# A recurrent-memory transformer block on one core: streamed weights copied into contiguous pieces, small transfers on ACT's queue, whole-bank evictions

## The chip, the cores and the metric

One core of one Trainium2 chip. The metric is device time in microseconds (us), median of several executions. A ratio is the mean time of one kernel's runs over that of the other's runs of the same rounds, so it is not quite the ratio of the medians that are quoted.

Engines: PE does matmuls, PEld its weight loads, ACT (ScalarE), DVE (VectorE) and POOL (GpSimd) the rest; SP issues transfers. "ACTq" and "SPq" are the issuing sequencers of ACT and SP. The profile counts 16 DMA engines. A bank is here a tile of 512 columns in PSUM, into which PE's matmuls add up; to evict it is to copy it out, so that the next instructions can read it.

## The reference

```python
def reference(A_x, A_mem0, A_Wq, A_Wk, A_Wv, A_Wo, A_seg_len, B_x, B_w1, B_b1, B_w2, B_b2):
    # x: 2048 x 1024, 32 heads of 128, 8 memory rows, segments of 32 rows -> 64 segments
    def _A_ref(x, mem0, Wq, Wk, Wv, Wo, seg_len):
        mem = mem0
        for s in range(n_seg):
            h = jnp.concatenate([mem, xs], axis=1)       # 8 + 32 rows
            q, k, v = h @ Wq, h @ Wk, h @ Wv             # each weight 1024 x 4096, 8 MB
            p = _softmax(masked(q @ k.T * scale))
            o = (p @ v) @ Wo                             # 4096 x 1024, 8 MB
            mem = o[:, :M, :].copy()                     # the next segment needs it
            outs.append(o[:, M:, :])
        ...
    def _B_ref(x, w1, b1, w2, b2):
        return gelu(x @ w1 + b1) @ w2 + b2               # 1024 -> 3584 -> 1024
    xn = _layernorm(A_x)
    return A_x + _A_ref(xn, ...) + _B_ref(xn, ...)
```
(Shortened; everything is bf16.) The four weights of A have 32 MB together, more than fits on chip with the rest. The kernel keeps 43 of 64 units of 512 KB resident and reads the other 21 again in each of the 64 segments.

## The kernel before

First the feed-forward block B for all 2048 rows in four token groups, with the layer norm; it leaves x + B in DRAM (`R_d`, and `RL_d` for the last 8 rows of each segment). Then the loop over segments. In it a segment is computed for 24 of its rows and the 8 memory rows; the leftover 8 rows of four segments are collected, so in each group of four the first segment also has their K and V, the fourth their O and the next group's Q. The 16 extra stores of their output go out during the next group's first segment. (The prediction and some expectations, which counted from the stores, call this one the "fourth" kind; the tables here call it the first.)

```python
        def unit_tile(unit):
            if IS_STREAMED[unit]:
                t = stp.tile([P, 2048], BF16, name="st")[:, :]      # 4 buffers
                fetch(t, unit)                   # SP; from the weight itself
                state["n"] += 1
                if state["n"] == STREAM_BUFS:
                    for fn in later:             # small loads and stores, SP too
                        fn()
                    later.clear()
                return t
            # [... resident units ...]

        def load_h(s):
            hT = sp.tile([P, KT, SEG], BF16, name="hT", bufs=2)
            nc.sync.dma_start(out=hT[:, :, :], in_=xT_d[:, s, :].rearrange("p (k t) -> p k t", k=KT))
            return hT
        # [... load_hL, load_res, load_resL alike ...]

        def copy2(dst, src):
            nc.scalar.copy(out=dst[0], in_=src[0])
            nc.vector.tensor_copy(out=dst[1], in_=src[1])
        # [...]
            for w in ("K", "Q"):
                left = left_kv if w == "K" else left_q
                for u in range(2):               # a half pass: 8 units into one PSUM bank
                    ps, psL = half_pass(w, u, left, {3: todo})
                    nat = evict(ps, [sp.tile([P, 256], BF16, name=nm) for nm in NAT[u]])  # copy2 of two halves
                    todo = [turner(nat, "kT" if w == "K" else "qT", u)]    # PE transposes, next half pass
        # [... scores, softmax, V, O; then, of a segment's output ot: ...]
            def store(s=s, ot=ot):
                for jq in range(4):
                    nc.sync.dma_start(
                        out=out_flat[s * SEG:s * SEG + NX, 256 * jq:256 * jq + 256], in_=ot[32 * jq:32 * jq + NX, :]
                    )
            later.append(store)                  # every fourth segment 16 more, store_left
```

The streamed unit of K, Q or V is 128 rows of 4 KB at a pitch of 8 KB; a unit of O is two blocks of 128 rows of 2 KB.

The softmax here doesn't subtract the row's maximum and nothing guards it: scores larger than these inputs give would overflow.

## Time and profile before

| | before |
|---|---|
| time, median | 3075.97 us (3052.85 to 3080.03) |
| span of the profiled run | 3067.4 us |
| block B, handover, loop | 454, 28, 2585 us |
| loop: DMA share, GB/s, mean clock | 0.83, 280, 0.87 |
| segment, by place in its group of four | 44.0, 37.9, 37.3, 41.9 us |
| DMA idle in it | 11.6, 4.4, 4.4, 6.8 us |

A page line of 40 digits cuts the span into equal slices, each digit the busy share in tenths. In the views of waits a row is engine, line, what it waited for, us in total, times, longest. The view of one engine in order of time has start, us, engine, line, operation and number. Segment figures are averages over the stretches between two additions of a segment's output (`ot`), so they start in the O pass of one segment and end in that of the next. The packets' durations come from the trace's own records of DMA packets. The prediction shows the lines of before and reads them.

### The profile page before, as it was taken

To read this page: it belongs to the slowest core of one execution; us is meant where nothing else is said; L and a number is where in the kernel's file an instruction comes from. 1 tells how busy PE (TensorE), PEld (TensorE's weight loads), DVE (VectorE), ACT (ScalarE), POOL (GpSimd) and SP (SyncE) were. 2 spreads that over 40 slices of the span, in tenths; PEclk is the share of its full clock that TensorE was granted. 3 is DMA by queue.
4 is the path that set the end of the run, shared out by engine and by line. 5 is a ranking of instruction groups with operands and counts; after the bars stand their busy time and mean duration, and the time that the engine had idled before them with its cause. 6 is when DMAs were issued, how large, how long until landed. Compare 5 with 4: busy or idle time off the path is not lost.

```text
span 3067.4 us, 83824 instructions
## 1 busy us (share of the span) xinstructions
PE 2197.4 (72%) x37364; PEld 1117.2 (36%) x37387; DVE 694.9 (23%) x2203; ACT 579.8 (19%) x1520; POOL 8.7 (0%) x28
## 2 busy tenths in 40 slices
PE   5899995676766676767666766767676776776775
PEld 2344442333333333433333333434333333333333
DVE  4566421111111111111111111111111111111111
ACT  2244221111111111111111111111111111111111
POOL 0000000000000000000000000000000000000000
PEclk9999997897888889888888798998888988888888
DMA  7111267878787878888787878787978887888787
GB/s 244 47 40 44 76 224 259 293 252 291 261 289 260 288 257 301 278 280 295 271 294 249 294 263 313 259 303 255 307 262 301 272 306 253 306 269 299 259 299 256
DMA packets 307206, 779.91 MB, mean 254 GB/s; under 512 B 32667, under 2 KB 78747, under 8 KB 306332
## 3 DMA queue, kind: packets, MB, share of 16 engines
q1 hardware_dynamic: 306716, 774.53, 75.0%
q8 instruction: 292, 4.78, 0.6%
q14 instruction: 70, 0.57, 0.1%
q10 hardware_dynamic: 128, 0.02, 0.0%
HBM read 759.72 MB, written 14.68 MB: 252 GB/s over the span
## 4 chain that ended last, share of the span: by engine, by line
DMA 47%; PE 39%; SPq 5%; DVE 4%; ACT 3%; issue 2%; POOL 0%; DVEq 0%; ACTq 0%; POOLq 0%
DMA st<-in_A_Wk_dram 20%; PE acc L509 17%; DMA st<-in_A_Wv_dram 17%; PE sm L681 7%; DMA st<-in_A_Wq_dram 5%; PE ps L293 5%; PE ps L339 5%; DMA st<-in_A_Wo_dram 4%; SPq L712 2%; PE tr L451 1%; PE ps L366 1%; PE acc L652 1%; ACT rc L622 1%; DVE kv L435 1%; ACT sm L619 1%
## 5 line engine op out<-in xcount | busy, mean ns | idle before, releaser
L509 PE MATMUL acc<-st,hT 128*32 128x512 bf16 x4096 | 470.4, 444 | 580.6 <-DMA st<-in_A_Wk_dram 372.0
L509 PE MATMUL acc<-W,hT 128*32 128x512 bf16 x8192 | 793.1, 436 | 0.4 <-issue 0.4
L509 PEld LDWEIGHTS <-hT 128*32 128x32 bf16 x12288 | 363.9, 103 | 1051.3 <-issue 846.6
L509 PE MATMUL acc<-W,hL 128*32 128x512 bf16 x2048 | 220.9, 413 | 0.8 <-issue 0.8
L293 PE MATMUL ps<-xnT,w 128*128 128x512 bf16 x896 | 199.5, 385 | 17.9 <-ACT g_xb L301 16.9
L435 DVE CAST natD<-acc 128x256 bf16<-128x256 f32 x192 | 80.8, 421 | 504.5 <-ACT natC L434 503.2
L434 ACT CAST natA<-acc 128x256 bf16<-128x256 f32 x192 | 71.4, 372 | 562.7 <-PE acc L509 477.1
L435 DVE CAST natB<-acc 128x256 bf16<-128x256 f32 x192 | 81.5, 424 | 399.4 <-ACT natA L434 347.5
L434 ACT CAST natC<-acc 128x256 bf16<-128x256 f32 x192 | 71.8, 374 | 493.2 <-PE acc L509 492.8
L339 PE MATMUL ps<-w,gT 128*128 128x512 bf16 x654 | 150.8, 386 | 5.5 <-ACT g_xb L301 2.5
L293 PEld LDWEIGHTS <-w 128*128 128x128 bf16 x896 | 88.7, 99 | 127.8 <-issue 25.6
L509 PEld LDWEIGHTS <-hL 128*32 128x32 bf16 x3072 | 92.8, 104 | 81.1 <-issue 25.8
L509 PE MATMUL acc<-st,hL 128*32 128x512 bf16 x1024 | 111.1, 414 | 0.5 <-issue 0.5
L435 DVE CAST kv<-acc 128x256 bf16<-128x256 f32 x128 | 53.9, 421 | 242.6 <-ACT kv L434 234.9
L435 DVE CAST o_sb<-sm 128x128 bf16<-128x128 f32 x63 | 18.4, 291 | 398.5 <-ACT o_sb L434 398.5
L652 PE MATMUL acc<-pr,kv 32*128 32x40 bf16 x2048 | 53.7, 179 | 63.4 <-DVE pr L623 42.8
L339 PEld LDWEIGHTS <-gT 128*128 128x128 bf16 x672 | 66.3, 99 | 85.9 <-issue 3.3
L681 PE MATMUL sm<-st,natA 128*32 128x256 bf16 x1024 | 71.0, 334 | 31.2 <-ACT natA L434 30.8
L681 PE MATMUL sm<-W,natB 128*32 128x256 bf16 x1536 | 91.1, 331 | 0.0
L434 ACT CAST o_sb<-sm 128x128 bf16<-128x128 f32 x63 | 16.7, 265 | 392.1 <-PE sm L681 392.1
L301 ACT ACTIVATE g_xb<-ps,b1col 128x512 bf16<-128x512 f32 x112 | 76.5, 683 | 67.7 <-PE ps L293 67.4
L434 ACT COPY kv<-tr 128x256 bf16<-128x256 bf16 x128 | 47.6, 372 | 220.1 <-PE tr L451 220.1
(118 smaller groups left out, 2420.3 us busy)
## 6 DMA issues: line engine op xcount, KB each, us to landing
st<-in_A_Wk_dram SPq DMA_DIRECT2D x384, 512.0 KB
st<-in_A_Wq_dram SPq DMA_DIRECT2D x320, 512.0 KB
st<-in_A_Wv_dram SPq DMA_DIRECT2D x320, 512.0 KB
st<-in_A_Wo_dram SPq DMA_DIRECT2D x320, 512.0 KB
w<-in_B_w_dram SPq DMA_DIRECT2D x14, 1024.0 KB
W<-in_A_Wq_dram SPq DMA_DIRECT2D x11, 512.0 KB
W<-in_A_Wv_dram SPq DMA_DIRECT2D x11, 512.0 KB
W<-in_A_Wk_dram SPq DMA_DIRECT2D x10, 512.0 KB
```

The lines of the kernel that those rows point to most:

```text
L293: nc.tensor.matmul(ps[:, :].rearrange("p (s t) -> p s t", t=SEG), lhsT=w1_sb[fb // 4][:, kt, (fb % 4) * P:(fb % 4 + 1) * P], rhs=xnT[:, :, ...
L301: nc.scalar.activation(out=xb[:, :], in_=ps[:, :], func=ACT.Identity, bias=b1col[:, fb:fb + 1], scale=1.0)
L339: nc.tensor.matmul(ps[:, :], lhsT=gts[fc // 7][:, fc % 7, t * P:(t + 1) * P], rhs=w2_sb[fc // 4][:, fc % 4, cs], start=(fc == 0), stop=(fc ...
L366: nc.tensor.matmul(pss[2 * t + nb][:, :], lhsT=gts[fc // 7][:, fc % 7, t * P:(t + 1) * P], rhs=w2_sb[fc // 4][:, fc % 4, nb * 512:nb * 512 ...
L434: nc.scalar.copy(out=dst[0], in_=src[0])
L435: nc.vector.tensor_copy(out=dst[1], in_=src[1])
L451: nc.tensor.transpose(dst[k][:, c, :], nat[k][:, c * P:(c + 1) * P], ident[:, :])
L509: nc.tensor.matmul(acc[32 * j:32 * j + 32, :], lhsT=lhs[:, i, :], rhs=t[:, 512 * j:512 * j + 512], start=(i == 0), stop=(i == KT - 1), til ...
L619: nc.scalar.activation(out=dA, in_=dA, func=ACT.Ln)
L652: nc.tensor.matmul(oV[j][:, c, :], lhsT=V[c // 2][q, (c % 2) * P:(c % 2 + 1) * P], rhs=prA[q, c, :], start=(c == 0), stop=False, skip_grou ...
L681: nc.tensor.matmul(psX[32 * jq:32 * jq + 32, o:o + 256], lhsT=lhs[:, c, :], rhs=t[:, 1024 * k + 256 * jq:1024 * k + 256 * jq + 256], start ...
L712: nc.sync.dma_start(out=rows_o[i, NX:SEG, 256 * jq:256 * jq + 256], in_=otL[32 * jq + NL * i:32 * jq + NL * i + NL, :],)
```

## The change

Its intent: read the streamed units from contiguous memory, keep SP's queue for the stream alone, evict a bank with one engine, and take work out of the first token group.

```diff
+    copies = {
+        unit: dram.tile([P, 2048], BF16, name="Wc_" + ...) for unit in ORDER if IS_STREAMED[unit]
+    }
 # [... at the end of the first token group ...]
+                if tg == 0:
+                    for unit, c in copies.items():
+                        fetch(c[:, :], unit)
 # [... the stream ...]
             if IS_STREAMED[unit]:
                 t = stp.tile([P, 2048], BF16, name="st")[:, :]
-                fetch(t, unit)
-                state["n"] += 1
-                if state["n"] == STREAM_BUFS:
-                    for fn in later: ...
+                nc.sync.dma_start(out=t, in_=copies[unit][:, :])
 # [... load_h, load_hL, load_res, load_resL, store, store_left: nc.sync -> nc.scalar ...]
-            nc.sync.dma_start(out=hT[:, :, :], in_=xT_d[:, s, :]...)
+            nc.scalar.dma_start(out=hT[:, :, :], in_=xT_d[:, s, :]...)
 # [... one engine for a bank: K, Q, second V and memory by ACT; first V and leftovers by DVE ...]
-                    nat = evict(ps, [sp.tile([P, 256], BF16, name=nm) for nm in NAT[u]])
+                    nat = sp.tile([P, 512], BF16, name=f"nat{u}")
+                    nc.scalar.copy(out=nat[:, :], in_=ps[:, :])
+                    if (w, u) == ("K", 0):
+                        for fn in later:
+                            fn()
+                        later.clear()
 # [... block B: residual stored by rows, turned later by DRAM-to-DRAM transfers ...]
         def keep_R(ttg, rsb):
-            for i in range(4): ...        # 8 small stores a tile
+            eng = nc.scalar if ttg >= NT - 4 else nc.sync
+            eng.dma_start(out=R_n[ttg * P:ttg * P + P, :], in_=rsb[:, :])
 # [... layer-norm statistics of later rows no longer loaded and computed in the first group ...]
-                if tg == 0 and fb >= 3 and fb % 2 and 4 + fb // 2 - 1 < NT:
-                    ln_stats(tt, load_x(tt, "xst", 2))
```

## The prediction

> **What bounds the kernel now.** I read the page's 40 slices first, to separate stages, then busy time by stretch, then the waits, the groups, the chain that ended last, and the queue of SP in order of time.
>
> ```profile
> PE   5899995676766676767666766767676776776775
> DMA  7111267878787878888787878787978887888787
> q1 hardware_dynamic: 306716, 774.53, 75.0%
> DMA 47%; PE 39%; SPq 5%; DVE 4%; ACT 3%; issue 2%; POOL 0%; DVEq 0%; ACTq 0%; POOLq 0%
> ```
>
> Two stages show: up to slice 6 (about 460 us) PE is at 8 or 9 tenths and DMA nearly idle, the feed-forward block and layer norm; after it DMA is at 7 or 8 tenths all the way, the recurrent loop over 64 segments, each of which reads 21 weight units of 512 KB again. By stretch (us, busy of PE, PEld, DVE, ACT, POOL, clock, DMA share, GB/s):
>
> ```profile
> 0.00:454.00 454.00, 408.13 (x1908) 187.04 (x1931) 234.39 (x581) 151.86 (x241) 8.68 (x28) 0.97 0.35 111
> 454.00:482.00 28.00, 0.53 (x2) 0.21 (x2) 3.64 (x9) 0.00 (x0) 0.00 (x0) 0.57 0.68 193
> 482.00:3067.00 2585.00, 1788.77 (x35454) 929.98 (x35454) 456.89 (x1615) 427.97 (x1279) 0.00 (x0) 0.87 0.83 280
> ```
>
> 454 us of block, 28 us of handover in which PE does nothing, 2585 us of loop. In the loop DMA is busy 83%; the waits of PE in it say whether it is the bound:
>
> ```profile
> PE acc L509 <- DMA st<-in_A_Wk_dram: 372.0, 205, 8.4
> PE acc L509 <- DMA st<-in_A_Wv_dram: 120.0, 177, 3.0
> PE acc L509 <- DMA st<-in_A_Wq_dram: 73.1, 92, 2.3
> PE acc L652 <- DVE pr L623: 42.8, 63, 0.8
> PE sm L681 <- DMA st<-in_A_Wo_dram: 41.8, 46, 2.4
> ```
>
> 607 us of waits for streamed units, and over half of that at K, the first thing of a segment. Why K: SP's queue in order of time around one segment start (start us, us, engine, line, transfer):
>
> ```profile
> 1497.49 3.97 SPq L163 DMA_DIRECT2D st<-in_A_Wk_dram  x4
> 1502.61 1.75 SPq L699 DMA_DIRECT2D out_dram<-ot  x4
> 1504.41 0.35 SPq L414 DMA_DIRECT2D hT<-xT_d  x1
> 1505.05 0.35 SPq L424 DMA_DIRECT2D res<-R_d  x1
> 1506.31 0.32 SPq L419 DMA_DIRECT2D hL<-xL_d  x1
> 1507.67 1.87 SPq L163 DMA_DIRECT2D st<-in_A_Wk_dram  x2
> ```
>
> After four stream issues SP waits for the last segment's output, issues small stores and loads, and only at 1507.67 goes on with the stream; in 1506-1509.5 the DMA share is 0.50. Every fourth segment adds 16 small stores of about 0.33 us each. I cut the loop at the output additions and averaged by position in the group of four: segments last 44.0 (K and V of leftover rows, 16 extra stores), 37.9, 37.3 and 41.9 us (leftover Q and O), at DMA shares 0.735, 0.883, 0.881, 0.837, so DMA stands idle 11.6, 4.4, 4.4 and 6.8 us of them. PE waits for DMA 9.95, 10.3, 10.1 and 8.2 us; what is left, 34.0, 27.6, 27.2 and 33.7 us, is PE's own path with its other waits.
>
> **What the Trainium skill says.** (1) "DMA: Bandwidth & Descriptors", section "Issuing engines are not separate DMA queues": transfers started by scalar or sync run on the same 16 engines, and a second issuer saves only issue time. The trace agrees on the cost: 0.28 to 0.43 us of queue time per small transfer; here that time is on the path. (2) The same page, "Latency and other measured facts", says that a large power-of-two row pitch lowers the rate; its smallest pitch is 512 KiB, the K, Q and V units have 8 KB, so it only hints. The trace decides: its packet records give the 4096-byte packets a median of 159 ns but a mean of 192 in the loop (a tail over 300 ns); the 2048-byte packets of O, contiguous in memory, a median of 84 and, where no other weight flows, a mean of 91.4. Excess over the median is 9% for O, 19% for K, Q, V (189 ns alone). (3) "PSUM — Partial Sum Buffer", section "PSUM bank collisions raise a hardware error": two engines must not touch the same bank and quadrant together, so accesses are serialised. The trace agrees: two half evictions of one bank run one after the other, ACT 1507.05 for 0.37 us, then DVE 1507.46 for 0.42, 0.83 in all. (4) "TensorE: Matmul & The Clock Gate", Part 1: idle halves the clock. The trace agrees: stretches at 0.50, loop mean 0.87.
>
> **The change, part by part.**
> *Contiguous pieces.* The 21 units are copied once to contiguous memory, 4096 bytes a row. O's packets become 4 KB as well. If the new packets have O's relative tail, one takes 159 x 91.4/84 = 173 ns. A segment has 21 x 128 = 2688; on 16 engines 2688 x 173/16 = 29.1 us. Before: 16 x 128 x 192/16 + 5 x 256 x 94.8/16 = 24.6 + 7.6 = 32.2 us. Saving 3.1 us, on the path where DMA is the bound. Small transfers stay, about 1 us: 30.1 us of DMA a segment.
> *Copying.* 11 MB DRAM to DRAM, queued behind the loads of the first token group, in a stage where the share is 0.1 to 0.2. At half the loop's 340 GB/s (an estimate) 65 us, hidden before the next token group needs anything.
> *Small transfers on ACT's queue.* SP issues nothing but the stream, so the next unit goes out when PE frees its buffer. Of the idle DMA time, I take 2.5 us in ordinary segments, and about 7 in the fourth with its 23 issues x 0.33 = 7.6 us. Cost: 6 to 22 issues on ACT, 2 to 7 us per segment, right after the first K eviction; ACT is 17% busy in the loop and has the next half pass (about 4 us) before it is needed. In the fourth segment the second K eviction may come 3 us late; four buffers of 1.4 us each cover that.
> *Evictions.* ACT or DVE alone takes a bank of 512 columns. ACT's activation of 128x512 takes 0.69 us, against 0.83 for the serial pair: 0.15 to 0.25 us sooner at K, Q, V and at the memory hand-back. Perhaps 0.5 us of PE's path a segment, mostly behind DMA.
> *The first stage.* The 12 extra loads and statistics in the first token group go. Now DVE waits 21 us for them and PE stands from 47 to 60, then runs at DVE's pace to 111; elsewhere the same 28 blocks take 48 us (158 to 205). Starting at about 21 instead of 23, the group ends at 70 instead of 111: 40 us. Statistics of later groups (4 x 1.4 us on DVE) go beside 12 us of matmuls; the later transposes cost about 1 us three times. Net 37 us.
> *The handover.* 32 small stores of the residual (0.3 us each on SP) become 4 stores now and the rest later: additions 5 us, one store's landing, a few issues, a 2 us landing, two transposes: about 14 instead of 28 us.
>
> **Sum.** Block and handover: 482 - 37 - 14 = 431 us. Ordinary segments: DMA 30.1 plus some 1.7 left idle = 31.8 us. The two with leftovers: PE's own path, 33 to 34 now, less about 1 for evictions and a higher clock, plus some remaining DMA wait: 34.5 us, DMA and PE nearly level there. Mean 33.2. First segment 38, 63 x 33.2 = 2092, tail 8: span 2569. Times ran some 9 us above the span (3075.97 against 3067.4): 2578, which I round to 2580.
>
> **The rivals.**
> *The layout brings nothing*: the tail belongs to the 16 engines, not to the 8 KB pitch. For it: some K/Q/V stretches already reach 380 to 397 GB/s, O has a tail too. Then DMA is 2688 x 189/16 + 1 = 32.8, ordinary segments 34.5, the others 36.3, mean 35.4: 139 us more, 2715.
> *PE becomes the bound everywhere*, since its queue of waits and half-clock stretches takes over: for it, 34 us of own path in two of four segments; against, 27 in the other two. With contiguous packets at the 159 ns median, DMA needs 27.7 us, and segments fall only to 29.5 and 33.5, mean 31.5: 2470.
> *ACT becomes the obstacle*: issues block its in-order queue (single issues took up to 1.8 us on SP[...]), evictions come late and PE waits 2 us a segment more: +120 us at most, about 2700.
> *The gain is hidden anyway*: against it stands that every part concerns the wait that ends last in the loop.
>
> **Range and chances.** The rate of contiguous packets moves the result by -110 to +139 us, ACT's issues by up to +120, the first stage by 20 either way. They hardly add up: 2450 to 2720. All rivals stay more than 11% under 3076, so slower or same would need a fault that nothing here shows: faster 0.97.
>
> **What will show it.** Packet records: mean of streamed 4 KB packets near 173 ns (159 to 180 right, 189 the first rival). Loop DMA share above 0.9 and over 325 GB/s. SP's queue without gaps of small issues at the segment start; PE's wait at K far under 372 us. Segment lengths near 32, 32, 34.5, 34.5. The loop starting near 431 us. Waits of PE for ACT's evictions over 2 us a segment would speak for the third rival. The prediction fails if the copies lie badly in memory (packets slower than 192 ns), or if the clock falls under 0.85.

## More of the kernel before

One more detail is needed later, two evictions of one bank of 512 columns in order of time:

```profile
1514.36 0.37 ACT L434 CAST natC<-acc 128x256 bf16<-128x256 f32 x1 [5.16 <-PE acc L509]
...
1514.77 0.43 DVE L435 CAST natD<-acc 128x256 bf16<-128x256 f32 x1 [5.24 <-ACT natC L434]
```

DVE starts when ACT has ended: 0.84 us for a bank.

## The result, and the profile after

| | before | after |
|---|---|---|
| time, median of 4 | 3078.0 us | 2896.77 us (2891.56 to 2903.1) |
| ratio | | 0.9429 (95%: 0.9374 to 0.9484) |
| span | 3067.4 us | 2889.8 us |

Faster by 5.7%, but 177 us above the top of the predicted range. (Before was run once more beside it, hence 3078.0.) The same parts of the page:

```profile
PE   7999986566776677767676777677676767677766
...
DMA  9401378869898888988887889887989787888987
...
q1 hardware_dynamic: 230124, 769.52, 75.9%
...
DMA 49%; PE 42%; ACT 3%; DVE 2%; issue 2%; ACTq 1%; SPq 0%; DVEq 0%
```

SP's queue is gone from the chain that ended last (5% to 0), and the packets of queue 1 are fewer (306716 to 230124), as O's units now have 4 KB rows and the small transfers left. The stages:

```profile
0.00:420.50 420.50, 400.77 (x1911) 185.30 (x1931) 236.29 (x586) 157.42 (x249) 10.78 (x28) 1.00 0.44 146
420.50:440.70 20.20, 0.52 (x3) 0.14 (x2) 4.09 (x8) 1.28 (x1) 0.00 (x0) 0.59 0.80 270
440.70:2889.00 2448.30, 1724.84 (x35454) 905.20 (x35454) 387.00 (x1103) 350.59 (x831) 0.00 (x0) 0.88 0.85 296
```

The block and the handover end at 441 us instead of 482, about as predicted (431). The loop is where the forecast fell: 2448 us instead of some 2138, at a DMA share of 0.85, not over 0.9. PE's waits in it:

```profile
PE tr L455 <- ACT nat L552: 157.8, 30, 13.1
PE acc L511 <- DMA st<-Wc_Q: 145.6, 123, 4.0
PE acc L511 <- DMA st<-Wc_K: 127.4, 184, 2.3
PE acc L511 <- DMA st<-Wc_V: 76.6, 119, 2.1
PE acc L649 <- DVE pr L620: 42.8, 63, 0.8
PE sm L679 <- DMA st<-Wc_O: 40.7, 59, 2.0
```

The wait at K fell from 372 to 127 us. Two others took part of its place: the wait at Q doubled (73.1 to 145.6), and a wait of the transposes for ACT's eviction of K appeared, in 30 cases up to 13 us each. ACT in order of time at the start of a group's first segment shows what it does instead:

```profile
1369.05 0.59 ACT L552 CAST nat<-acc 128x512 bf16<-128x512 f32 x1 [4.14 <-PE acc L511]
1369.12 1.58 ACTq L697 DMA_DIRECT2D out_dram<-ot  x4
1372.46 9.51 ACTq L710 DMA_DIRECT2D out_dram<-ot  x16
1382.01 0.37 ACTq L424 DMA_DIRECT2D hT<-xT_d  x1
1382.42 0.71 ACTq L434 DMA_DIRECT2D res<-R_d  x1
1383.23 0.59 ACT L552 CAST nat<-acc 128x512 bf16<-128x512 f32 x1 [13.60 <-DMA out_dram<-ot]
```

Between the evictions of K's first and second half lie 22 issues, 14 us in place of the 7.3 that 22 issues of 0.33 us would take. In 1376 to 1383 PE does nothing. SP's queue, which now has nothing but the stream, in the same stretch:

```profile
1366.19 1.61 SPq L414 DMA_DIRECT2D st<-Wc_K  x2
1368.78 11.40 SPq L414 DMA_DIRECT2D st<-Wc_Q  x5
```

Five issues of 0.3 to 0.5 us each are spread over 11.4 us. Averages by place in the group:

| segment | us before | us after | DMA idle before | after | PE waits for ACT's eviction, after |
|---|---|---|---|---|---|
| first (leftover K, V; 16 more stores) | 43.96 | 42.63 | 11.65 | 11.09 | 8.53 |
| second | 37.91 | 36.22 | 4.45 | 3.33 | 0.85 |
| third | 37.33 | 35.13 | 4.43 | 3.62 | 0.47 |
| fourth (leftover Q, O) | 41.93 | 38.49 | 6.81 | 4.98 | 0.53 |

The idle DMA time that was to go is mostly still there. PE's waits for ACT's eviction are 157.8 us over 63 segments, 2.5 us each; over 2 was what the prediction named as the sign of its third rival. And the 4096-byte packets of the stream have a mean of 184.8 ns (192.1 before), not 173; 8.9% of them last over 1.25 of the median of 159 ns (12.9% before).

Why should SP still stand still, when it issues only the stream? The instruction list of the built program names what each instruction waits for (an excerpt, with SP's and ACT's rows from different places; the traces agree with it, see below):

```
SP:  667 st_18368<-Wc_Q_5_0_104 128x2048         [waits DMAHW5_49,DMAHW0_49,PE_49]
SP:  668 st_18385<-Wc_Q_0_1_105 128x2048         [waits DMAHW6_49,DMAHW1_49,PE_49]
ACT: 589 out_0_dram<-ot_12807 24x256             [waits DMAHW3_49,DVE_49]
ACT: 590 out_0_dram<-ot_12807 24x256             [waits DMAHW5_49]
ACT: 593 hT_12854<-xT_d_57 128x256               [waits DMAHW1_49]
```

A semaphore is a counter on which one instruction can wait until another has finished. In this built program the transfers complete on eight semaphores, DMAHW0 to DMAHW7, which the transfers of both queues use in turn. A transfer on SP waits until an earlier one on the same semaphore has landed, even if that one was issued on ACT; and ACT's wait for SP's. The trace shows the same: in the loop, SP's stream and ACT's small transfers complete on the same eight semaphores (numbers 101 to 105 and 107 to 109). In the trace of the changed kernel SP's waits in the loop contain

```profile
SPq L414 <- PE acc L511: 589.4, 713, 6.3
SPq L414 <- PE sm L679: 337.2, 297, 4.2
SPq L414 <- DMA st<-Wc_K: 211.3, 159, 4.5
SPq L414 <- DMA st<-Wc_Q: 208.3, 191, 5.4
SPq L414 <- DMA out_dram<-ot: 191.3, 83, 5.9
```

191 us of SP's waits ended with the landing of a small store. By place in the group such waits for small transfers are 7.7, 2.0, 4.8 and 2.4 us per segment; before, at most 0.2.

Not all of this waiting is loss, as SP would wait for a free buffer meanwhile. So, from the trace, how long a stream issue starts after both its buffer was free (PE's last matmul on the unit four loads back) and SP's previous stream issue was over: of 1336 issues 133 start more than 0.3 us late, 281 us together. 127 of them start within 0.15 us of a landing on the very semaphore that they use. ACT is held likewise: of its 136 pauses of 0.3 to 6 us before an issue, 131, 155 us together, end within 0.15 us of such a landing, and 70 of these landings belong to SP's stream.

**Theory A**: the slow packets belong to restarts of the stream after gaps, so the layout is worth little. **Theory B**: the two queues are coupled, by the shared semaphores and by ACT's order, in which evictions stand behind issues; that is where the expected gain went. **Rivals**: (C) the loop simply runs at the stream's own rate and PE's own path; (D) ACT's order alone is the obstacle.

### The profile page after: what moved, and what is told of

It is laid out like the page before. It is cut to its first block, busy times and chain, and to the rows that moved or that the text cites. A ratio compares the mean times of both kernels' runs of the same rounds, so it can differ in the third digit from the quotient of the medians. Undisturbed runs are those within 1.5% of the kernel's fastest.

```text
span 2889.8 us, 82618 instructions
## 1 busy us (share of the span) xinstructions
PE 2126.1 (74%) x37367; PEld 1090.6 (38%) x37387; DVE 627.4 (22%) x1696; ACT 509.3 (18%) x1081; POOL 10.8 (0%) x28
## 3 DMA queue, kind: packets, MB, share of 16 engines
q1 hardware_dynamic: 230124, 769.52, 75.9%
## 4 chain that ended last, share of the span: by engine, by line
DMA 49%; PE 42%; ACT 3%; DVE 2%; issue 2%; ACTq 1%; SPq 0%; DVEq 0%
PE acc L511 15%; DMA st<-Wc_Q 15%; DMA st<-Wc_V 13%; DMA st<-Wc_K 11%; PE sm L679 9%; PE ps L306 7%; DMA out_dram<-ot 5%; PE ps L353 5%; DMA st<-Wc_O 2%; PE tr L455 2%; PE ps L382 1%; PE acc L649 1%; ACT rc L619 1%; ACT oT L663 1%; ACT sm L616 1%
## 5 line engine op out<-in xcount | busy, mean ns | idle before, releaser
L511 PE MATMUL acc<-W,hT 128*32 128x512 bf16 x8192 | 763.8, 422 | 1.2 <-issue 1.2
L511 PE MATMUL acc<-st,hT 128*32 128x512 bf16 x4096 | 452.5, 428 | 372.1 <-DMA st<-Wc_Q 145.6
L552 ACT CAST nat<-acc 128x512 bf16<-128x512 f32 x256 | 150.1, 586 | 1242.2 <-PE acc L511 835.0
L679 PEld LDWEIGHTS <-oT 128*32 128x32 bf16 x8192 | 251.2, 109 | 132.3 <-issue 70.7
L455 PE MATMUL tr<-ident,nat 128*128 128x128 bf16 x1024 | 113.6, 241 | 158.2 <-ACT nat L552 157.8
L679 PE MATMUL sm<-W,oT 128*32 128x256 bf16 x4096 | 223.4, 315 | 3.3 <-issue 3.2
L679 PE MATMUL sm<-st,oT 128*32 128x256 bf16 x2560 | 165.5, 313 | 76.0 <-DMA st<-Wc_O 40.7
L533 DVE COPY kv<-tr 128x512 bf16<-128x512 bf16 x128 | 54.3, 424 | 651.0 <-PE tr L455 651.0
L455 PEld LDWEIGHTS <-nat 128*128 128x128 bf16 x1024 | 64.6, 105 | 280.5 <-ACT nat L552 192.0
L533 DVE COPY qT<-tr 128x512 bf16<-128x512 bf16 x128 | 54.3, 425 | 432.8 <-PE tr L455 432.8
L598 ACT ACTIVATE pr<-sm 128x448 bf16<-128x448 f32 x64 | 34.8, 544 | 298.6 <-PE sm L593 298.6
```

The costliest lines, as they stand in the source:

```text
L455: nc.tensor.transpose(dst[:, c, :], nat[:, c * P:(c + 1) * P], ident[:, :])
L511: nc.tensor.matmul(acc[32 * j:32 * j + 32, :], lhsT=lhs[:, i, :], rhs=t[:, 512 * j:512 * j + 512], start=(i == 0), stop=(i == KT - 1), til ...
L533: nc.vector.tensor_copy(out=dst[:, :, 0:32], in_=by_head(tr[:, :, :]))
L552: nc.scalar.copy(out=nat[:, :], in_=ps[:, :])
L598: nc.scalar.activation(out=pr, in_=psS[:, 0:448], func=ACT.Exp, scale=INV_SQRT_DH)
L679: nc.tensor.matmul(psX[32 * jq:32 * jq + 32, o:o + 256], lhsT=lhs[:, c, :], rhs=t[:, 1024 * k + 256 * jq:1024 * k + 256 * jq + 256], start ...
```

## The experiments

Each was timed in 3 rounds beside the kernel before, in four series on four chips; the kernel before had medians of 3075 to 3078 us in all four. Differences between two changed kernels are differences of their medians; the 95% intervals of the ratios correspond to 7 to 17 us either way. Names with "pool" have the small transfers on GpSimd.

### One part undone: no copies

```diff
-                nc.sync.dma_start(out=t, in_=copies[unit][:, :])
+                fetch(t, unit)
```
(and the copying removed)

> The changed kernel with one part undone: the stream reads the 21 units from the original weights again, there are no copies. Theory A (the tail of slow packets belongs to the moments in which the stream starts again after a gap, not to the layout): the mean of the 4096-byte packets in the loop stays between 180 and 195 ns, and only O pays for its 2048-byte packets; 20 to 80 us more than the changed kernel's 2897 us. Rival, as predicted (contiguous pieces save 3.1 us a segment): about 200 us more, near 3095 us. First stage unchanged, loop start at 440 us within 5.

Measured: 3054.09 us, 157 us more than the changed kernel (ratio to before 0.9915, 0.9877 to 0.9953). Packets of 4096 bytes 194.4 ns, those of 2048 bytes 94.1. Every kind of segment is longer by 2 to 3 us. The packets alone would have fitted theory A (180 to 195 ns), but its 20 to 80 us do not: theory A falls, and the layout is worth about four fifths of what was predicted for it (3.1 us a segment, 198 us). Part of it is packet time: 16 x 128 x 194.4/16 + 5 x 256 x 94.1/16 = 32.4 us a segment against 2688 x 184.8/16 = 31.0, so some 90 of the 157 us. The rest is not explained.

### One part undone: small transfers back on SP

```diff
-            nc.scalar.dma_start(out=hT[:, :, :], in_=xT_d[:, s, :]...)
+            nc.sync.dma_start(out=hT[:, :, :], in_=xT_d[:, s, :]...)
```
(likewise all small loads and stores of the loop)

> The changed kernel with one part undone: the small loads and stores of the loop are issued on SP again, at the places in the program where the changed kernel has them. Theory B (the move gained little, because in the built program both queues share eight completion semaphores in rotation, so SP's stream waits for the small transfers that ACT issues late, and ACT's evictions wait behind its issues): within 2% of the changed kernel, 2840 to 2950 us; the waits of PE for the eviction of K's second half fall from 8.5 us to under 2 us in every fourth segment, and DMA waits come in their place. Rival, as predicted (SP free of small issues saves 2.5 us in three segments and 7 in the fourth): 230 us more, near 3130 us.

Measured: 2992.45 us, 95 us more than on ACT. That misses theory B's 2%, and is far from the predicted 230. Segments 45.8, 36.4, 36.5, 40.3 us; no waits for ACT's evictions, PE's waits for DMA 12, 10, 10 and 7 us. So ACT's queue did bring something, less than half of the forecast. By the measure from above 70 stream issues start late, by 463 us together, and 408 us of this end when DVE has added up the output that the stores on SP's queue wait for. It is no exact return to before: the small transfers now come after three stream issues of the segment, formerly after four.

### Small transfers on GpSimd

```diff
-            nc.scalar.dma_start(out=hT[:, :, :], in_=xT_d[:, s, :]...)
+            nc.gpsimd.dma_start(out=hT[:, :, :], in_=xT_d[:, s, :]...)
```
(likewise the other small loads, the stores and the last turned residuals)

> The changed kernel with the loop's small loads and stores issued on GpSimd, whose transfers have eight completion semaphores of their own in the built program, so that neither SP's stream nor ACT's evictions wait for them. Theory B: segments fall from 42.6, 36.2, 35.1, 38.5 us to about 34, 32, 32, 34; time 2600 to 2700 us; waits of PE for ACT's eviction under 1 us in every kind of segment. Rival C (the loop is at the rate of the stream itself, packets of 185 ns and PE's own path): no more than 60 us less than the changed kernel, 2840 to 2900 us.

In the built program the small transfers now wait on other semaphores, DMASW0 to DMASW7, and the stream on DMAHW alone; in the trace GpSimd's transfers complete on numbers 111 to 118, the stream on its old eight. Measured: **2688.45 us**, ratio to before 0.8750 (0.8701 to 0.8799). Segments 34.8, 34.0, 32.7 and 36.8 us; DMA idle 3.6, 1.7, 1.8 and 3.7. The loop in the view by stretch:

```profile
441.00:2680.00 2239.00, 1656.69 (x35456) 889.37 (x35456) 387.78 (x1104) 349.95 (x831) 358.05 (x699) 0.94 0.91 324
```

SP's waits in the same kernel's loop:

```profile
SPq L414 <- PE acc L511: 621.1, 886, 3.4
SPq L414 <- PE sm L679: 343.5, 296, 3.7
SPq L414 <- DMA st<-Wc_K: 231.1, 282, 5.4
SPq L414 <- DMA st<-Wc_Q: 181.3, 254, 2.7
```

No row of this view is left for a small transfer. PE's waits for ACT's evictions of K and Q are gone too. DMA is busy 91% at 324 GB/s, PE's mean clock rose to 0.94. Rival C falls: the stream can go much faster than in the changed kernel. Of 1336 stream issues 1 now starts more than 0.3 us late, by 1.3 us (133 and 281 us in the changed kernel). This is the best of the kernels here that compute the right result, and it lies inside the range that was predicted for the changed one.

### ACT's order without the coupling of semaphores, step by step

```diff
-                    nc.scalar.copy(out=nat[:, :], in_=ps[:, :])
+                    if (w, u) == ("K", 1):            # e12: in (("K", 1), ("Q", 0))
+                        nc.vector.tensor_copy(out=nat[:, :], in_=ps[:, :])
+                    else:
+                        nc.scalar.copy(out=nat[:, :], in_=ps[:, :])
```

> The changed kernel, with K's second bank evicted by DVE instead of ACT, so that the issues on ACT no longer stand before that eviction, while the shared semaphores stay. Theory B (both count): PE's wait of 8.5 us for the eviction in every fourth segment goes, but SP's stream still waits for the small transfers, so DMA waits come in its place: 20 to 80 us less than the changed kernel. Rival D (ACT's order alone is the obstacle): 15 segments x 8 us plus some tenths in the others, 120 us or more less, under 2780 us.

Measured: 2838.17 us, 59 us less than the changed kernel. In the first segments PE still waits 3.4 us for ACT, now for Q's first half. So, with both on DVE:

> The changed kernel with K's second and Q's first bank evicted by DVE, so that PE needs nothing of ACT while it issues the small transfers; they stay on ACT and in the shared rotation of semaphores. Theory B: PE's wait for ACT's evictions falls under 1 us in the fourth kind of segment (3.4 us with K's second bank alone on DVE), and what remains over the kernel on GpSimd is the rotation: segments of 37 to 39, 35.5, 35, 38 us, time 2780 to 2835 us. Rival D (ACT's order alone): within 2% of 2688 us.

Measured: 2828.86 us (2805.27 to 2836.53). PE's waits for evictions of K or Q on ACT are 0.2 us in the first segments and none in the others. Segments 38.7, 36.1, 34.9, 38.6 us against 34.8, 34.0, 32.7, 36.8 on GpSimd. SP's waits in its loop still have the row

```profile
SPq L414 <- DMA out_dram<-ot: 203.3, 89, 5.7
```

and SP waits 9.3, 2.1, 4.8 and 1.7 us per segment for small landings. Rival D falls: of the 208 us between ACT's queue and GpSimd's, 68 go when PE no longer needs ACT's evictions of K and Q; 140 us remain. The 68 are net: with ACT's order out of the way, the stream was held longer than before, 168 issues late by 343 us together.

### Only the 16 extra stores on GpSimd

```diff
-                            nc.scalar.dma_start(
+                            nc.gpsimd.dma_start(
                                 out=rows_o[i, NX:SEG, 256 * jq:256 * jq + 256],
```

> The changed kernel with only the 16 small stores of the leftover rows issued on GpSimd; the 4 stores and 2 or 3 loads of each segment stay on ACT. Theory B: the fourth kind of segment falls from 42.6 to about 36.5 us, since only 6 issues stand before the eviction and in the rotation; the other three, which keep the shared semaphores, stay at 36, 35 and 38.5 us, not at the 34, 32.7 and 36.8 of the kernel wholly on GpSimd: 16 x 6 = 96 us less, 2780 to 2820 us. Rival: the 16 stores are the whole matter: under 2720 us.

Measured: 2796.37 us. The first segment falls from 42.6 to 35.9 us; the others stay at 36.1, 35.2 and 38.4. As expected by B: 6 or 7 small transfers on ACT still cost each of the other segments some 2 us over GpSimd's queue.

### Small transfers issued earlier on ACT

```diff
             todo = []
+            for fn in later:
+                fn()
+            later.clear()
             for w in ("K", "Q"):
```
(and removed behind K's first half pass)

> The changed kernel with the small transfers placed ahead of K's first half pass instead of behind it; all stay on ACT, which issues them some 3 us earlier and is idle then. Theory B (rotation of eight shared semaphores): now the third prefetched unit of the next segment, and those behind it, wait for stores that wait for the end of this segment, so the prefetch is cut: the ordinary segments get longer by 2 us or more (36.2 and 35.1 to over 38), the time goes over 2990 us. Rival E (what is left of the loss on ACT's queue is that both issuers share the making of descriptors, or the rings, not the semaphores): earlier issue does no harm, 2800 to 2900 us.

Measured: 2888.06 us, the same as the changed kernel within 0.3%; segments 43.3, 35.7, 34.5, 39.1. My expectation of theory B was wrong (over 2990 us), and the time is the one that was written down for rival E, something else that both issuers share, such as the rings or the making of descriptors. SP's waits for small landings are 8.5, 1.7, 1.5 and 3.9 us per segment, 241 us in all against 261: the stores are issued earlier, and what that gives at one place is lost at another. So the time of this run does not tell B's semaphores from E.

The traces do tell more. If the rings or the descriptors were what two issuers share, the stream's transfers should take longer once issued. They do not: from issue to landing their mean is 5.3 us in the changed kernel and with two evictions on DVE, 5.5 on GpSimd's queue. GpSimd's own small stores even take longer than ACT's, 4.8 us against 3.7 on average, so its gain is not that they are faster. What differs is when the stream's issues may start: late by 281 us in the changed kernel, 343 with two evictions on DVE, 197 here, and 1.3 on GpSimd, nearly all ended by a landing on the semaphore to be used. So the coupling by semaphores is shown; how many of the 140 us each late issue costs stays open, as the lateness and the time do not go in step. A kernel that keeps ACT's queue but gives it its own semaphores could not be built here.

### One part alone, on the kernel before

```diff
-            nc.sync.dma_start(out=hT[:, :, :], in_=xT_d[:, s, :]...)
+            nc.gpsimd.dma_start(...)                  # e8;  e14: nc.scalar
```
(in the kernel before, all small transfers of the loop, at their old place)

> The kernel before, with the one part of moving the loop's small loads and stores off SP, but to GpSimd instead of ACT. The prediction's term for this part was 2.5 us in three segments and 7 in the fourth, 232 us: 2846 us. If SP's small issues were not what held the stream: over 3000 us.

> The kernel before, with the one part of moving the loop's small transfers to ACT's queue, at their old place in the program. Theory B: the rotation stays shared, so little of the 216 us that GpSimd's queue brought comes: 2960 to 3080 us. The prediction's step (SP issues nothing but the stream): 2846 us, as on GpSimd.

Measured: 2860.18 us on GpSimd and **3122.53 us on ACT**, before 3075.28 and 3077.30. The predicted value of freeing SP's queue was 232 us; GpSimd's queue gives 215. ACT's queue, taken alone, makes the kernel 1.4% slower (1.0144, 1.0111 to 1.0178): clear of noise, and above the 2960 to 3080 us that I expected. In its first segments PE waits 11.5 us for copies on DVE that stand behind copies on ACT, which stand behind issues:

```profile
PE tr L451 <- DVE kv L435: 171.9, 39, 11.0
```

In the kernel before, this row has 25.1 us.

### The evictions

```diff
-                    nc.scalar.copy(out=nat[:, :], in_=ps[:, :])
+                    halves(nat, ps, 256)              # ACT the first 256 columns, DVE the others
```
(likewise V, the leftovers, the memory and the copies of the transposes)

> The kernel on GpSimd's queue, with every bank of 512 columns (and the memory hand-back) evicted in two halves by ACT and DVE again, as before the change, and the transposes copied out by both. As predicted, half a us of PE's path a segment, mostly behind DMA: 10 to 35 us more than 2688. Rival: the serial pair is on the path of the segments with leftovers, which are PE's: 60 us or more.

Measured: 2704.06 us, 16 us more than with whole banks, as predicted for this part. But it is within the noise of two kernels in different series (ratios 0.8788 and 0.8750, with intervals that overlap), so no gain is shown.

### What the layout does

> The kernel with small transfers on GpSimd (2688 us), with the copies undone: the stream reads the original weights. What the layout is worth where nothing else holds the stream. From the packets (192 to 194 ns and 94 ns before, 182 to 185 after) it is 1.4 us of DMA a segment, 90 us: 2780 us. If it is worth what it was in the changed kernel (157 us): 2845 us. If the prediction's 3.1 us a segment held: 2885 us. If the layout matters only where the stream restarts after gaps: under 2740 us.

> The same kernel on GpSimd's queue, with only O's five units copied, K, Q and V from the original weights at 8 KB pitch. If the gain of the layout is O's (256 pieces of 2 KB become 128 of 4 KB): within 30 us of 2688. If it is K's, Q's and V's tail of slow packets: within 30 us of the kernel without copies. K, Q, V packets then keep a share of about 13% over 1.25 of the median, against 7.5% where they are copied.

Edits: the first undoes the copies in the kernel on GpSimd's queue; the second keeps those of O:

```diff
-        unit: dram.tile(...) for unit in ORDER if IS_STREAMED[unit]
+        unit: dram.tile(...) for unit in ORDER if IS_STREAMED[unit] and unit[0] == "O"
# [... the stream fetches the other units from the weights ...]
```

Measured: 2801.57 us without copies, 2795.47 us with O's alone, against 2688.45 with all. O's larger packets bring 6 us, within the noise; the 107 us come from K, Q and V. Where the stream is not held up, the layout is thus worth 113 us. The 4096-byte packets: 189.3 and 188.2 ns, against 182.3 with all copied, 10% slow ones in place of 7.5%. (I had expected 13%.)

> The kernel on GpSimd's queue, with the copies laid out in rows of 8 KB of which the stream reads the first 4 KB, so that the pieces have the pitch of the original K, Q and V. If the pitch makes the slow packets: mean 187 to 191 ns, time near the 2795 us of the kernel in which only O was copied. If it is where the original weights lie: within 25 us of 2688.

> Wrong result on purpose: the kernel on GpSimd's queue, but every streamed transfer reads the first copied piece, so the stream stays within one 512 KB stretch of DRAM. If the remaining tail of slow packets (7.5% over 1.25 of the median, mean 182 ns) belongs to where in memory the pieces lie: mean under 172 ns, time under 2620 us. If it belongs to the engines or to starts of transfers: mean 178 to 186 ns, within 2% of 2688 us.

```diff
-        unit: dram.tile([P, 2048], BF16, ...)          # e11: the rows 8 KB apart
+        unit: dram.tile([P, 4096], BF16, ...)
-                nc.sync.dma_start(out=t, in_=copies[unit][:, :])
+                nc.sync.dma_start(out=t, in_=copies[unit][:, 0:2048])
```
```diff
-                nc.sync.dma_start(out=t, in_=copies[unit][:, :])      # e9: always the first piece
+                nc.sync.dma_start(out=t, in_=copies[ORDER[0]][:, :])
```

Measured: 2896.97 us with the pitch of 8 KB, 209 us more than contiguous; packets 188.8 ns, DMA idle 5.2, 3.8, 3.7 and 6.5 us (3.6, 1.7, 1.8, 3.7). So copying the weights to another place is not enough: the gain goes with the contiguous rows. (With the pitch the stretch of memory that the pieces span doubles; the two were not separated.) I had expected some 2795 us in this case. It costs even more than the originals do (2802): the packets are as slow there, the idle time is not as long; why is open. With always the same piece 2685.82 us and 184.2 ns, nothing gained: the tail that is left, 7.5 to 8% of the packets, does not belong to where in memory the pieces lie. (This kernel computes with wrong weights. The attention's part of the output is small beside x, which is my reading and was not tested; so the check on values says little of this part.)

## Why the prediction was wrong

By its own steps:

- **The bound, and what SP's issues cost: right.** DMA is the bound of the ordinary segments, and small issues on SP held the stream: 215 us by a run that frees SP (2860.18), 232 predicted. Segments fell by 7.8, 2.3, 1.6 and 2.6 us there, 7 and three times 2.5 predicted.
- **"SP issues nothing but the stream, so the next unit goes out when PE frees its buffer": this step failed.** On ACT's queue the next unit also waits until small transfers have landed, on semaphores that both queues share (133 issues late by 281 us), and ACT's evictions wait behind its issues. Segments came out at a mean of 38.04 us, predicted 33.2; over 63 segments that is 305 us, nearly all of the 320 us by which the span missed. Of these, 3.47 x 63 = 219 us go when GpSimd issues (mean 34.57).
- **The cost on ACT: right in kind, wrong in size.** The text named "ACT becomes the obstacle", at most 120 us, and counted up to 22 issues in 7 us; they took 14 us, since issues wait for landings. "Four buffers cover that" was wrong: PE stood for 8.5 us in each first segment. In the changed kernel ACT's order accounts for 68 us, by the run with two evictions on DVE. So this rival kept within its 120 us; the other 140 belong to a coupling that no rival named.
- **Packets at 173 ns: mis-sized.** 184.8 ns were measured, 182.3 without the coupling. The extrapolation from O's packets was wrong: contiguity does not remove the tail that all packets have. At 2688 packets on 16 engines, 9.3 ns more (182.3 against 173) are 1.6 us a segment, some 98 us where DMA is the bound (an estimate); this would cover the 86 us by which even the kernel on GpSimd's queue lies over the predicted segments ((34.57 - 33.2) x 63). The rival "the layout brings nothing" was wrong as well: it brings 113 to 157 us.
- **The segments with leftovers** were both put at 34.5 us, as PE's own path with a rest of DMA wait. The parts forecast before do not add up to this: 44.0 - 3.1 - 7 = 33.9 and 41.9 - 3.1 - 2.5 = 36.3. On GpSimd's queue they take 34.8 and 36.8, of which PE waits 3.1 and 5.3 for DMA, so the parts were right and the second 34.5 too low.
- **The first stage: right.** FFN and norm of the first group end with PE busy 49.95 of 50 us from 22 to 72; the stage ends at 420.5 (417 implied by 454 - 37). The handover took 20 us, not 14. With the first segment this makes the loop's first addition come at 483.8 us, not 469: the other 15 of the 320 us.
- **The copying: right,** hidden: from 22 to 90 us PE is busy 67.89 of 68 us, beside a DMA share of 1.03 in the view.
- **The evictions:** right in size for one, 0.59 us for a bank in place of 0.84; 16 us in all, which noise does not let one confirm.
- **The range** treated the rivals as alternatives ("They hardly add up"). ACT's order (68 us) and slower packets (86 us) came together, and with them the coupling, which was not among them (140 us). That GpSimd's queue gives a time inside the range, 2688 us, does not confirm the sum: its packets were slower than forecast, and it is another change.

## What to carry to other kernels

A second queue is free only if nothing that it issues waits for another queue: look up in the built program which semaphores its transfers wait on, and in the trace which landings the issuer waits for, before counting on a second queue. Do not put issues on an in-order engine that also evicts banks that PE needs; here an otherwise idle engine with semaphores of its own made 208 us of difference. And when weights are read many times, try one contiguous copy: here, with weights at a pitch of only twice the row, it brought 113 and 157 us, and the copying was hidden.

## What the Trainium skill lacked or had wrong

- "DMA: Bandwidth & Descriptors", section "Issuing engines are not separate DMA queues", says that a second issuer saves only issue time, usually little. Here the choice of the issuer of transfers that are 2% of DMA's time is worth 304 us: 2992 us on SP, 2897 on ACT, 2688 on GpSimd. What the issuer decided was when the stream's issues could start. No page says that transfers of SP and ACT may share completion semaphores in a built program and so wait for one another.
- The same page, section "Issuing engine by pattern", gives simple loads and stores to Sync and calls the hardware path of sync and scalar generally faster. For small loads and stores beside a stream GpSimd was better by 208 us than scalar, though its small stores took longer to land (4.8 us on average against 3.7).
- The same page's row on power-of-two pitches in "Latency and other measured facts" starts at 512 KiB, for copies between tensors in HBM. Loads with a pitch of 8 KB and rows of 4 KB already cost 209 us here (2896.97 against 2688.45), with packets of 188.8 against 182.3 ns.
- None has it: SBUF-bound 4 KB packets that are contiguous in DRAM have a tail of 7.5% over 1.25 of their median (159 ns), which stays when one 512 KB piece is read again and again (8%).
